# Mamba2 scan and SwiGLU feed-forward on one core: scan outputs of every second 64 tokens written with swapped feature halves, and a new order of steps

## The chip, the cores and the metric

One core of one Trainium2 chip runs the whole program. The metric is device time in microseconds (us). Engines are named as in the profile: PE is TensorE (matrix products, with PEld its weight loads), DVE is VectorE, ACT is ScalarE, POOL is GpSimd, SP is SyncE, which issues the DMAs here. Each engine executes its own instructions in the order in which the program emits them, and semaphores order the engines among each other.

## The reference, cut to what matters

```python
# x: 4 batches, 8 heads, 768 tokens, 32 features; a: decays; B, C: 16 states; chunks of 32
log_a = np.log(np.clip(a, 1e-06, 1.0))
...
    cum = np.cumsum(la, axis=-1)
    L = np.exp(cum[:, :, :, None] - cum[:, :, None, :]) * causal
    M = np.einsum('bhin,bhjn->bhij', Cc, Bc) * L
    y_intra = np.einsum('bhij,bhjd->bhid', M, xc)
    y_inter = np.einsum('bhin,bhnd->bhid', Cc, state) * np.exp(cum)[:, :, :, None]
    y[:, :, sl] = y_intra + y_inter
    state = decay_full * state + np.sum(Bx, axis=2)
...
# y as 3072 tokens x 256 features, then
rms = np.sqrt(np.mean(x * x, axis=-1, keepdims=True) + 1e-06)
xn = x / rms * rms_g
g = xn @ w_gate              # 256 x 1536
silu = g * (1.0 / (1.0 + np.exp(-g)))
return silu * (xn @ w_val) @ w_out
```

## The kernel before

**Scan.** The 768 tokens of a sequence are worked on in chunks of 64; two chunks (u = 0 and 1, 64 tokens each) make 128 tokens, and a *pair* p is two such groups (i = 0, 1), 256 tokens. There are 12 pairs and 6 *blocks* of 512 tokens (TB), so a block is two pairs. For a pair, `turn`/`turned` (L498, L514) transpose B and C, `product` (L549) multiplies C with B into g, a masked decay L is built from row and token sums (`spread` L457 by DMA, `subtract` L464, `exponential` L471, `decayed` L597), `additions` (L619) computes what the tokens add to the state (A) and `states` (L634) carries the state S on. The outputs of pairs 0 and 1 come from `first_outputs` (L658), those of all later pairs from `outputs` (L689), whose matmuls are recorded at L699. `outputs` has two stages: first C times the state ("T,S" in the profile: tiles of 32 rows by 64 columns, one for each q, that is two heads' 32 state rows, at row group 32q), then L times x ("L,xr": 64 rows by 32 columns, one for each head, row half by u). Before the change the result stands in four PSUM banks: y[2k+u] holds feature half k (128 of 256 features, one on each partition) of chunk u; the banks of k = 0 form one tile (the "y pair"), those of k = 1 are two single banks y2 and y3. The matmuls of the next pair's `additions` (`after`, "xr,Bd", L627) follow into the same banks.

**Norm.** `squares` (L733) squares y on ACT and adds the halves on POOL; `taken_out` (L751) copies y to SBUF on ACT (the copies are recorded at L763); `norm_sums` (L769), `norm_roots` (L781: Ln, then Exp, then a DMA), `spread_roots` (L792: four DMAs) and `norm_apply` (L799) make the normed tokens xn; in blocks after the first, `combine_x` (L883) makes sums of its quarters, tx.

**Feed-forward.** The weights come as float64 words (`fetch` L149, 20 pieces), and are decoded by ACT (`power` L175), DVE (`mantissa` L189) and DVE again (`weight` L198). In block 0 the first tiles of gate and value are plain products (`products_early` L831, `products_gv` L822). The rest goes by seven products in the place of eight, a tile j of 256 hidden features at a time: `product_gv` (L893) does product P.k of tile j, two matmuls of 128x256; products 1, 6, 7 and 4 accumulate in one PSUM buffer of the gate (two such buffers), 2, 5 and 3 in one of the value. After each of P.1, P.6, P.7, ACT copies the gate buffer (`taken_gv` L915, recorded at L917) before the next of them may write there; `total_gv` (L920, recorded at L923) adds copy and value buffer on DVE, `silu_gv` (L925) and `hide_gv` (L934) make the hidden features, and `product_o` (L982, recorded at L1001), `taken_o` (L1012) and `total_o` (L1019) project them with w_out, again by seven products.

**Order.** The loop over blocks is not in the code: the string `order` (L1193 to L1349) lists every step of the program, "block:kind.arguments/slot", some 1,500 of them, and the loop at L1350 executes it. Kinds are bound to functions in `first_kinds` (block 0) and `kinds` (later blocks, where the scan steps such as `y`, `sq`, `yt`, `ms`, `rs`, `xn` act on the block after). In the prediction's text `P`, `take`, `C`, `silu`, `hid` are the steps of the seven products, `o` and `O` of the projection, `pow`, `man`, `wt` of decoding the piece of that number, `row` the sums of four chunks' decays (`row_sums` L1072), `rowe` their exponent (e_sb, L1089), `turn`, `T`, `Tt` the transposition of a pair, and `table` and `exps` preloads of ACT's function table (Silu, or Ln with Exp). ACT also loads a table by itself where the next function needs another set; the profile shows that as ACT_TABLE_LOAD.

## Time and profile before

| what | value |
| --- | --- |
| three runs | 403.33, 405.25, 405.29 us (median 405.25) |
| span of the profiled execution (its own time is not listed apart from it) | 402.1 us |
| busy: PE, DVE, ACT, POOL | 394.8, 297.9, 224.5, 37.6 us |
| one pass of a 128x128 by 128x256 matmul (L911), mean of a record | 0.38 us |
| copy of a gate buffer (L917), 99 of them | 0.581 us mean |
| sum on DVE (L923), 99 of them | 0.688 us mean |
| table loads on ACT | 21 of 1.283 us |
| DMA moved | 26.99 MB |

The span is the profiled execution from its first to its last instruction. An fp32 matmul leaves two records, one for each pass. The record of a matmul is longer than the time by which the next may follow it, since they are pipelined: passes of 256 columns follow each other every 0.216 us, those of 128 every 0.11 us. "Idle before" in a group of instructions is what the engine stood still ahead of them, with the engine and line that released it.

### The profile page before, as it was taken

The page shows a single profiled execution, that of the slowest core. Times are in us where ns is not written, and L with a number is a line of the kernel's source. Part 1 is how long each engine was busy: PE and PEld are TensorE (multiplying, and loading weights), DVE is VectorE, ACT ScalarE, POOL GpSimd, SP SyncE. Part 2 cuts the span into 40 slices and gives each one's busy share as a digit, 9 for nine tenths or more (in the row PEclk, how much of TensorE's full clock was granted, in tenths as well). Part 3 has the DMA queues.
Part 4 walks back from the last instruction along what each step waited for, and adds up shares of the span by engine and source line. Part 5 has one row for each costly group of instructions (what it writes and reads, how often), then busy time and mean ns, then how long its engine had stood idle before and what let it go on. Part 6 is the DMA issues. An engine that isn't in the chain of part 4 may idle for free.

```text
span 402.1 us, 9591 instructions
## 1 busy us (share of the span) xinstructions
PE 394.8 (98%) x3881; PEld 338.9 (84%) x3881; DVE 297.9 (74%) x686; ACT 224.5 (56%) x456; POOL 37.6 (9%) x57
## 2 busy tenths in 40 slices
PE   8989999999999999999999999999999999999997
PEld 5656477888888899888899988899988899988996
DVE  6999999999477997567689467887555767366871
ACT  3989887894684362753572653482645551445410
POOL 2210010001300021200102300021200010000000
PEclk9999999999999999999999999999999999999999
DMA  9989997129012306301223700202000001100001
GB/s 110 189 248 277 178 183 236 38 42 96 2 39 67 68 22 118 79 0 17 68 74 80 104 2 0 44 30 71 27 2 2 2 9 54 52 0 2 0 2 52
DMA packets 92595, 26.99 MB, mean 67 GB/s; under 512 B 77288, under 2 KB 86376, under 8 KB 92552
## 3 DMA queue, kind: packets, MB, share of 16 engines
q1 hardware_dynamic: 88392, 26.13, 30.1%
q10 hardware_dynamic: 4160, 0.26, 0.8%
q8 instruction: 30, 0.49, 0.5%
q14 instruction: 13, 0.11, 0.1%
HBM read 22.64 MB, written 3.74 MB: 66 GB/s over the span
## 4 chain that ended last, share of the span: by engine, by line
PE 91%; SPq 3%; DMA 2%; DVE 1%; ACT 1%; issue 0%
PE gate L911 28%; PE o L1001 24%; PE val L911 21%; PE o L943 5%; PE gate L827 4%; PE y L699 3%; PE gate L837 2%; PE g L562 2%; SPq L121 1%; DMA wr<-in_moe_w_val_dram 1%; PE tp L505 1%; SPq L128 1%; DMA br<-in_B_dram 1%; PE y L627 1%; SPq L160 1%; PE ms L777 0%
## 5 line engine op out<-in xcount | busy, mean ns | idle before, releaser
L923 DVE TENSOR_TENSOR c<-val,p 128x512 f32<-128x512 f32 x99 | 67.5, 688 | 33.8 <-PE val L911 29.6
L917 ACT COPY p<-gate 128x512 f32<-128x512 f32 x99 | 57.4, 581 | 53.2 <-PE gate L911 50.4
L911 PE MATMUL gate<-tx,sw 128*128 128x256 f32 x264 | 65.8, 381 | 0.0
L932 ACT ACTIVATE c<-c 128x256 f32<-128x256 f32 x99 | 39.5, 416 | 44.5 <-DVE c L923 44.5
L911 PEld LDWEIGHTS gate<-tx,sw 128*128 128x128 f32 x264 | 49.5, 190 | 7.1 <-issue 0.3
L936 DVE TENSOR_TENSOR h<-c 128x256 f32<-128x256 f32 x99 | 41.1, 426 | 18.2 <-ACT c L932 18.2
L911 PE MATMUL val<-xn,sw 128*128 128x256 f32 x132 | 33.6, 382 | 0.5 <-DVE c L923 0.5
L911 PE MATMUL val<-tx,sw 128*128 128x256 f32 x132 | 33.6, 383 | 0.1
L911 PE MATMUL val<-xn,wgv 128*128 128x256 f32 x132 | 33.7, 382 | 0.0
L911 PE MATMUL gate<-xn,wgv 128*128 128x256 f32 x132 | 33.4, 380 | 0.0
L911 PE MATMUL gate<-tx,wgv 128*128 128x256 f32 x132 | 33.0, 381 | 0.0
L475 POOL TENSOR_SCALAR_AFFINE_SELECT L<-L 64x512 f32<-64x512 f32 x32 | 23.7, 740 | 87.0 <-ACT L L473 85.8
L1001 PE MATMUL o<-wo,h 128*128 128x128 f32 x240 | 29.9, 276 | 0.0
L1001 PEld LDWEIGHTS o<-wo,h 128*128 128x128 f32 x240 | 28.5, 192 | 0.5 <-issue 0.2
L1001 PE MATMUL o<-two,h 128*128 128x128 f32 x240 | 28.9, 276 | 0.0
L1001 PE MATMUL o<-two,s 128*128 128x128 f32 x240 | 28.9, 276 | 0.0
L911 PEld LDWEIGHTS val<-xn,sw 128*128 128x128 f32 x132 | 24.8, 190 | 4.2 <-DVE c L923 0.9
L1001 PEld LDWEIGHTS o<-two,s 128*128 128x128 f32 x240 | 28.0, 192 | 0.4 <-issue 0.2
L911 PEld LDWEIGHTS val<-tx,sw 128*128 128x128 f32 x132 | 24.7, 190 | 3.9 <-DVE c L923 0.5
L1001 PEld LDWEIGHTS o<-two,h 128*128 128x128 f32 x240 | 27.8, 192 | 0.2 <-DVE s L967 0.2
L911 PEld LDWEIGHTS gate<-tx,wgv 128*128 128x128 f32 x132 | 24.8, 190 | 3.5 <-ACT c L932 0.2
L911 PEld LDWEIGHTS val<-xn,wgv 128*128 128x128 f32 x132 | 24.8, 190 | 3.5 <-issue 0.2
(188 smaller groups left out, 614.1 us busy)
## 6 DMA issues: line engine op xcount, KB each, us to landing
L<-rowd SPq DMA_DIRECT2D x32, 128.0 KB, 3.0
xr<-in_x_dram SPq DMA_DIRECT2D x24, 128.0 KB, 4.7
wr<-in_moe_w_out_dram SPq DMA_DIRECT2D x6, 512.0 KB, 7.0
wr<-in_moe_w_val_dram SPq DMA_DIRECT2D x5, 512.0 KB, 6.4
wr<-in_moe_w_gate_dram SPq DMA_DIRECT2D x5, 512.0 KB
out_dram<-ob SPq DMA_DIRECT2D x9, 256.0 KB, 2.2
br<-in_B_dram SPq DMA_DIRECT2D x22, 64.0 KB
cr<-in_C_dram SPq DMA_DIRECT2D x22, 64.0 KB, 2.4
```

Of the source, the lines that this page charges most:

```text
L475: nc.gpsimd.affine_select(out=L[r], in_=L[r], pattern=[[0, NH], [1, HC]], compare_op=ALU.is_ge, fill=0.0, base=0, channel_multiplier=-1)
L562: nc.tensor.matmul(out=g[u, P * i:P * i + P].rearrange("p (t m) -> p t m", t=2), lhsT=T[r, i, 0, u], rhs=T[r, i, 1:3, u], start=(first and ...
L699: nc.tensor.matmul(out=y[2 * k + u][rows, (2 * n + i) * HC:(2 * n + i + 1) * HC], start=(k, u, rows.start) not in opened, stop=True, skip_ ...
L827: nc.tensor.matmul(out=gv[:, k], lhsT=w[:, t, fs], rhs=xns[0][:, t], start=(t == 0), stop=(t == 1))
L837: nc.tensor.matmul(out=gv[:, k, tk], lhsT=w[:, t, fs], rhs=yts[0][:, t, tk], start=(s == 0 and t == 0), stop=(t == 1), skip_group_check=True)
L911: nc.tensor.matmul(out=dst[:, half[w]], lhsT=lhsT, rhs=rhs, start=(k in (1, 2, 5) and w == 0), stop=True, skip_group_check=True)
L917: nc.scalar.copy(out=t, in_=Xs[j])
L923: nc.vector.tensor_tensor(out=t, in0=Zs[j], in1=a, op=ALU.add)
L932: nc.scalar.activation(out=u, in_=src[:, half[0]], func=AF.Silu)
L936: nc.vector.tensor_tensor(out=hidden_tile(blk, j)[:, c // 10 - 1, c % 10 - 1], in0=u, in1=src[:, half[1]], op=ALU.mult)
L943: nc.tensor.matmul(out=o, lhsT=hs_[blk, f // 2][:, f % 2, k // 2, (k % 2) * P:(k % 2 + 1) * P], rhs=wo[:, f], start=opens, stop=(f == NF - ...
L1001: nc.tensor.matmul(out=o[t] if apart else o[:, t * P:(t + 1) * P], lhsT=lhsT[:, t], rhs=rhs, start=(k in (1, 2, 4, 5) and j == 0 and (apar ...
```

## The change

In `outputs` the four banks change places: now the two banks of u = 1 form the y pair, and those of u = 0 are y2 and y3. For u = 1 the column strip of the PE array, and with it the PSUM partitions, are swapped by halves of 64 in both stages, and in the first stage the loop over u goes inside the loop over q. `squares` and `taken_out` follow: three squares as before, the two single banks apart and the pair at once, into a tile sq with two planes (the square roots r now use its second plane, where they had a tile of their own); four copies in the place of three, since the pair is copied in two steps of 64 partitions each, from the other half. The sums of squares need no swap, since they run over all partitions and both banks. The rest of the diff is the order string: it holds the same 1,548 steps, but from the one behind `0:man.5` on (the 91st) they stand in a new order; only the last 238 steps, from the end of block 4 on, are as before. Of the string the lines up to the first products after 60 us are kept below, and two more that the prediction speaks of.

```diff
--- before.py
+++ after.py
@@ -691,7 +691,7 @@
         first = p - n
         if n == 0:
             ps["y pair", p] = pair
-            ps["y", p] = [pair[:, 0], pair[:, 1], bank("y2", (P, 512)), bank("y3", (P, 512))]
+            ps["y", p] = [bank("y2", (P, 512)), pair[:, 0], bank("y3", (P, 512)), pair[:, 1]]
         y, s, opened = ps["y", first], st[p], set()
         width = 1 if p < 4 else 2
 
@@ -702,11 +702,11 @@
             opened.add((k, u, rows.start))
 
         for i in range(2):
-            for u in range(2):
-                for q in range(NQ):
+            for q in range(NQ):
+                for u in range(2):
                     if (2 * p) % NC == 0 and i == 0 and u == 0:
                         continue
-                    r, o = slice(32 * q, 32 * q + 32), 64 * (q % 2)
+                    r, o = slice(32 * q, 32 * q + 32), 64 * ((q + u) % 2)
                     S = state[2 * (2 * p + i) + u - 1]
                     product_y(q // 2, u, i, slice(o, o + 64),
                               lhsT=S[r].rearrange("p t d -> p (t d)"),
@@ -715,7 +715,7 @@
         for i in range(2):
             for h in range(NH):
                 for u in range(2):
-                    o = 32 * (h % 4)
+                    o = 32 * ((h + 2 * u) % 4)
                     product_y(h // 4, u, i, slice(o, o + 32), lhsT=s["x"][halves[u], i, h],
                               rhs=Ls[p][halves[u], i, h], tile_position=(HC * u, o))
         for k, p2 in enumerate(after):
@@ -724,44 +724,50 @@
                            for u in range(2)])
         del st[p], Ls[p]
 
-    def parts_of_y(p):
-        y, n = ps["y", p], 2 if p < 4 else 4
-        cols = slice(0, n * HC)
-        return n, [(0, slice(0, 2), ps["y pair", p][:, :, cols])] + [
-            (1, slice(u, u + 1), y[2 + u][:, cols].unsqueeze(1)) for u in range(2)]
+    def columns_of_y(p):
+        n = 2 if p < 4 else 4
+        half = p % 2
+        return n, slice(half * 256, half * 256 + 256) if p < 4 else slice(0, TB), slice(0, n * HC)
 
     def squares(p):
         blk, half = divmod(p, 2)
         if half == 0:
-            sqs[blk] = nrm.tile([P, TB], FP32, tag="sq", name="sq", bufs=1)
-        tk = slice(half * 256, half * 256 + 256) if p < 4 else slice(0, TB)
+            sqs[blk] = nrm.tile([P, 2, TB], FP32, tag="sq", name="sq", bufs=1)
+        n, tk, cols = columns_of_y(p)
         if p < 2:
-            sq2 = nrm.tile([P, 2, 256], FP32, tag="sq2", name="sq2", bufs=1)
+            sq2 = sqs[blk][:, 1].rearrange("p (k m) -> p k m", k=2)
             nc.scalar.activation(out=sq2, in_=ps["y", p][:, :, 0:256], func=AF.Square)
-            nc.gpsimd.tensor_tensor(out=sqs[blk][:, tk], in0=sq2[:, 0], in1=sq2[:, 1], op=ALU.add)
+            nc.gpsimd.tensor_tensor(out=sqs[blk][:, 0, tk], in0=sq2[:, 0], in1=sq2[:, 1],
+                                    op=ALU.add)
             return
-        n, parts = parts_of_y(p)
-        sq2 = nrm.tile([P, 2 * n * HC], FP32, tag="sq2", name="sq2", bufs=1)
-        for k, us, y in parts:
-            dst = (sqs[blk][:, tk], sq2)[k].rearrange("p (j u m) -> p u j m", j=n, u=2)
-            nc.scalar.activation(out=dst[:, us],
-                                 in_=y.rearrange("p u (j m) -> p u j m", j=n), func=AF.Square)
-        nc.gpsimd.tensor_tensor(out=sqs[blk][:, tk], in0=sqs[blk][:, tk], in1=sq2, op=ALU.add)
+        dst = sqs[blk][:, :, tk].rearrange("p k (j u m) -> p k u j m", j=n, u=2)
+        y = ps["y", p]
+        for k in range(2):
+            nc.scalar.activation(out=dst[:, k, 0], func=AF.Square,
+                                 in_=y[2 * k][:, cols].rearrange("p (j m) -> p j m", j=n))
+        nc.scalar.activation(
+            out=dst[:, :, 1], func=AF.Square,
+            in_=ps["y pair", p][:, :, cols].rearrange("p k (j m) -> p k j m", j=n))
+        nc.gpsimd.tensor_tensor(out=sqs[blk][:, 0, tk], in0=sqs[blk][:, 0, tk],
+                                in1=sqs[blk][:, 1, tk], op=ALU.add)
 
     def taken_out(p, copy):
         blk, half = divmod(p, 2)
         if half == 0:
             yts[blk] = nrm.tile([P, 2, TB], FP32, tag="yt", name="yt", bufs=1)
-        tk = slice(half * 256, half * 256 + 256) if p < 4 else slice(0, TB)
+        n, tk, cols = columns_of_y(p)
         if p < 2:
             for t in range(2):
                 nc.vector.tensor_scalar(out=yts[0][:, t, tk], in0=ps["y", p][:, t, 0:256],
                                         scalar1=gcol[:, t:t + 1], scalar2=None, op0=ALU.mult)
             return
-        n, parts = parts_of_y(p)
-        for k, us, y in parts:
-            copy(out=yts[blk][:, k, tk].rearrange("p (j u m) -> p u j m", j=n, u=2)[:, us],
-                 in_=y.rearrange("p u (j m) -> p u j m", j=n))
+        dst = yts[blk][:, :, tk].rearrange("p k (j u m) -> p k u j m", j=n, u=2)
+        y = ps["y", p]
+        for k in range(2):
+            copy(out=dst[:, k, 0], in_=y[2 * k][:, cols].rearrange("p (j m) -> p j m", j=n))
+        pair = ps["y pair", p][:, :, cols].rearrange("p k (j m) -> p k j m", j=n)
+        for r, there in zip(halves, halves[::-1]):
+            copy(out=dst[r, :, 1], in_=pair[there])
 
 
     xns, roots = {}, {}
...
@@ -1199,153 +1205,152 @@
         0:Tt.0.1.1 0:exp.0.1 0:turn.0.0 0:Tt.0.1.0 0:T.0.0 0:sums.0.0 0:Tt.0.0.0 0:exp.0.0
         0:turn.1.1 0:T.1.1 0:scale.1 0:Tt.1.0.1 0:fetch.2 0:Tt.1.1.1 0:cc 0:g.0.1/1 0:L.0.1
         0:turn.1.0 0:Tt.1.1.0 0:Tt.1.0.0 0:sums.1.1 0:T.1.0 0:exp.1.1 0:A.0 0:S.0 0:A.1 0:S.1
-        0:g.0.0/0 0:man.0 0:pow.0 0:L.0.0 0:pow.1 0:wt.0 0:last.1 0:man.5 0:mask.1.0/1 0:middles
-        0:Tl.1 0:sums.1.0 0:never16 0:fetch.4 0:exp.1.0 0:g.1.0/2 0:fetch.3 0:x.4 0:L.1.0 0:last.0
-        0:Tl.0 0:scale.2 0:fetch.6 0:g.1.1/0 0:fetch.7 0:man.1 0:pow.5 0:L.1.1 0:y.0/1 0:wt.5 0:sq.0
-        0:fetch.12 0:row.1 0:pow.3 0:rowout.1 0:yt.0 0:ydone.0 0:rowe.1 0:y.1/2 0:r.1 0:fetch.13
-        0:row.0 0:man.2 0:fetch.9 0:wt.1 0:early.0.0/0 0:parts.1 0:man.6 0:mask.3/1 0:sums.3 0:pow.2
-        0:wt.2 0:rowe.0 0:dT.2 0:sq.1 0:ms.0 0:yt.1 0:ydone.1 0:early.0.1 0:man.3 0:wt.3 0:mask.2/2
-        0:sums.2 0:pow.6 0:fetch.8 0:wt.6 0:man.4 0:x.2 0:exp.3 0:early.1.0/1 0:rs.0 0:norm.0 0:xn.0
-        0:pow.4 0:wt.4 0:fetch.10 0:man.7 0:dT.3 0:turn.2 0:early.1.1 0:norm.1 0:rowout.0 0:exp.2
-        1:table 0:man.9 0:silu.0 0:hid.0 0:gate.2/0 0:T.2 0:Tt.2.0 0:Tt.2.1 0:Td.2 0:pow.7
-        0:fetch.14 0:wt.7 0:tx.0 0:gg.2/1 0:L1.2.2 0:L1.2.3 0:L.2.0 0:man.8 0:gate.3/2 0:pow.9
-        0:fetch.11 0:silu.2 0:hid.2 0:pow.8 0:wt.9 0:wt.8 0:man.11 0:silu.3 0:hid.3 0:A.2 0:S.2
-        0:x.3 0:pow.11 0:gate.4/1 0:silu.4 0:hid.4 0:cw.3 0:bc.3 0:scale.3 0:man.10 0:pow.12
-        0:gate.5/0 0:silu.5 0:hid.5 0:pow.10 0:y.2/2 0:S.3 0:yt.2 0:sq.2 0:ydone.2 0:switch.1
-        0:P.2.3 0:switch.0 0:P.1.3 0:take.1.3 0:turn.3 0:T.3 0:Tt.3.0 0:Tt.3.1 0:wt.10 0:wt.11
-        0:P.1.4 0:P.6.3 0:take.6.3 0:man.12 0:Td.3 0:man.13 0:pow.14 0:gg.3/2 0:L1.3.3 0:L.3.0
-        0:L1.3.2 0:bc.4 0:scale.4 0:P.2.4 0:P.7.3 0:bc.5 0:scale.5 0:x.5 0:y.3/2 0:wt.12 0:take.7.3
-        0:C.11.3 0:P.5.3 0:silug.11.3 0:pow.13 1:S.0 0:fetch.18 0:P.4.3 1:dT.0 0:C.22.3 0:P.3.3
-        0:take.1.4 0:silug.22.3 0:cw.4 0:P.6.4 0:silu.1 0:silug.21.3 0:C.11.4 0:silug.11.4
-        0:take.6.4 0:P.5.4 0:P.7.4 1:S.1 0:sq.3 0:yt.3 0:ydone.3 1:turn.1 0:tok 0:tokout 0:wt.13
...
+        0:g.0.0/0 0:man.0 0:pow.0 0:L.0.0 0:pow.1 0:wt.0 0:last.1 0:man.5 0:fetch.7 0:fetch.9
+        0:fetch.4 0:x.5 0:mask.1.0/1 0:sums.1.0 0:last.0 0:middles 0:g.1.0/2 0:exp.1.0 0:Tl.1
+        0:g.1.1/0 0:Tl.0 0:fetch.3 0:L.1.0 0:pow.5 0:y.0/1 0:sq.0 0:L.1.1 0:fetch.6 0:row.1
+        0:rowout.1 0:rowe.1 0:man.1 0:yt.0 0:fetch.11 0:r.1 0:pow.2 0:wt.1 0:y.1/2 0:wt.5 0:sq.1
+        0:pow.4 0:early.0.0/0 0:turn.2 0:T.2 0:parts.1 0:ms.0 0:rs.0 0:never16 0:mask.3/1 0:Tt.2.0
+        0:fetch.8 0:sums.3 0:man.2 0:exp.3 0:yt.1 0:row.0 0:x.2 0:man.3 0:xn.0 0:wt.2 0:early.0.1
+        0:man.4 0:pow.3 0:dT.2 0:scale.2 0:wt.3 0:mask.2/2 0:sums.2 0:exp.2 0:rowe.0 0:wt.4 0:bc.3
+        0:man.9 0:norm.0 0:pow.9 0:man.7 0:wt.9 0:pow.7 0:Tt.2.1 0:early.1.0/1 0:early.1.1 0:norm.1
+        0:fetch.10 0:ydone.1 0:gate.3/2 0:silu.0 0:man.6 1:dT.1 0:rowout.0 0:pow.6 0:Td.2 0:bc.5
+        0:gg.2/1 0:wt.7 0:silu.1 0:L.2.0 0:hid.0 0:L1.2.3 0:L1.2.2 0:ydone.0 0:gate.2/0 0:scale.3
+        0:A.2 0:pow.8 0:wt.6 0:gate.4/1 0:man.8 0:tx.0 0:wt.8 0:silu.2 0:hid.2 0:S.2 0:gate.5/0
+        0:pow.11 0:cw.3 0:silu.3 0:hid.3 0:x.3 0:y.2/2 0:silu.4 0:pow.10 0:fetch.14 0:man.10 0:hid.4
+        0:bc.4 0:man.11 0:S.3 0:silu.5 0:hid.5 0:switch.1 0:P.2.3 0:switch.0 0:scale.4 0:sq.2 0:dT.3
+        0:wt.11 0:fetch.12 0:yt.2 0:turn.3 0:scale.5 0:T.3 0:Tt.3.0 0:P.1.3 0:Tt.3.1 0:Td.3 0:gg.3/2
+        0:wt.10 0:L.3.0 0:L1.3.2 1:table 0:L1.3.3 0:take.1.3 0:P.6.3 0:fetch.13 0:pow.12 0:x.4
+        0:y.3/2 0:take.6.3 0:P.7.3 0:pow.14 0:P.1.4 0:man.12 0:C.11.3 0:cw.4 0:wt.12 1:S.0
+        0:take.7.3 0:silug.11.3 0:pow.13 0:P.5.3 0:C.22.3 0:P.4.3 0:silug.21.3 0:fetch.16 1:S.1
+        0:hidg.21.3 0:take.1.4 0:P.2.4 0:C.11.4 0:sq.3 0:P.3.3 1:dT.0 0:C.12.3 0:P.6.4 0:hidg.11.3
+        0:man.13 0:wt.13 0:man.14 0:yt.3 0:take.6.4 0:P.5.4 0:tok 0:pow.16 0:ydone.3 0:tokout
+        0:P.7.4 1:turn.1 0:fetch.18 0:take.7.4 0:C.22.4 0:silug.22.3 0:P.1.5 0:take.1.5 0:ms.1
+        0:spread.10 0:fetch.15 0:hidg.22.3 0:P.4.4 0:P.2.5 0:wt.14 0:silug.11.4 0:silug.21.4 0:P.3.4
+        0:hid.1 0:silug.12.3 0:silug.22.4 0:pow.15 0:ydone.2 0:o.0/2 0:cw.5 0:P.6.5 0:hidg.11.4
+        0:C.11.5 0:silug.11.5 0:spread.8 0:hidg.21.4 0:P.5.5 0:spread.11 0:hidg.12.3 1:T.1 1:Tt.1.0
+        0:o.1 0:fetch.17 0:hidg.22.4 0:table.1 0:hidg.11.5 0:take.6.5 0:man.15 0:wt.15 0:exps 1:cw.2
+        0:P.7.5 0:cw.1 0:rs.1 0:rb.1 0:o.2 0:o.3 0:take.7.5 0:C.22.5 0:P.3.5 0:man.16 0:silug.22.5
+        0:C.12.4 0:wt.16 0:P.4.5 0:spread.9 0:C.12.5 0:hidg.22.5 0:o.4 0:o.5 0:xn.1 1:P.1.0 0:cw.0
+        0:pow.17 0:silug.21.5 1:P.2.0 0:tx.1 1:turn.0 0:silug.12.4 0:pow.18 0:hidg.12.4 0:silug.12.5
...
+        4:P.1.0 3:Oadd.11 3:ex.2 4:P.2.0 3:Oadd.21 4:P.1.1 3:tx 4:take.1.0 4:P.6.0 4:C.11.0 3:exps
+        4:take.1.1 4:P.6.1 4:take.6.0 4:P.7.0 4:P.5.0 4:take.7.0 4:P.4.0 4:silu.21.0 3:O.3.0 3:s4.4
...
```

More of the change, by code (lines that the diff above doesn't have):

```diff
@@ L772, in norm_sums @@
             ps["m", blk] = ms = bank("ms", (P, TB))
-            nc.tensor.matmul(out=ms, lhsT=mean, rhs=sqs[blk], start=True, stop=True)
+            nc.tensor.matmul(out=ms, lhsT=mean, rhs=sqs[blk][:, 0], start=True, stop=True)
             return
@@ L1219 @@
-        0:take.1.4 0:silug.22.3 0:cw.4 0:P.6.4 0:silu.1 0:silug.21.3 0:C.11.4 0:silug.11.4
-        0:take.6.4 0:P.5.4 0:P.7.4 1:S.1 0:sq.3 0:yt.3 0:ydone.3 1:turn.1 0:tok 0:tokout 0:wt.13
-        0:take.7.4 0:fetch.15 0:fetch.16 0:C.12.3 0:silug.12.3 0:P.2.5 0:pow.15 0:ms.1 1:dT.1
-        0:P.4.4 0:man.14 0:hidg.22.3 0:hidg.11.3 0:hidg.21.3 0:P.1.5 0:silug.21.4 0:C.22.4
-        0:take.1.5 0:silug.22.4 0:P.3.4 0:wt.14 0:pow.16 0:o.0/2 0:hid.1 0:cw.5 0:P.6.5 0:o.1
-        0:fetch.17 0:man.15 0:C.11.5 0:take.6.5 0:P.5.5 0:table.0 0:fetch.19 0:hidg.11.4 0:hidg.22.4
@@ L1225 @@
-        0:hidg.12.3 0:P.7.5 0:C.12.4 0:silug.12.4 0:take.7.5 0:wt.15 0:pow.17 0:o.2 0:o.3 0:man.16
-        0:wt.16 0:o.4 0:o.5 0:cw.1 0:P.4.5 0:man.17 0:hidg.21.4 0:hidg.12.4 0:wt.17 0:o.6 0:o.7
-        0:man.18 0:C.22.5 0:P.3.5 0:exps 0:spread.10 0:spread.8 0:sub.8 0:spread.9 0:spread.11
-        0:sub.10 0:man.19 0:rs.1 0:rb.1 1:turn.0 0:silug.11.5 0:hidg.11.5 0:pow.18 0:wt.18 0:o.8
-        0:o.9 1:two.0 1:T.1 0:pow.19 0:wt.19 1:T.0 0:C.12.5 0:silug.12.5 0:sub.11 0:hidg.12.5 0:o.10
-        0:silug.21.5 0:hidg.21.5 0:silug.22.5 0:ex.11 0:xn.1 1:P.1.1 1:take.1.1 1:P.2.1 1:P.1.0
```

241 lines of the change are left out of this document (120 added, 121 removed).

## Prediction

> **What bounds the kernel now.** I read the page's first part, its slices and its chain first, to see which engine carries the end.
>
> ```profile
> span 402.1 us, 9591 instructions
> ## 1 busy us (share of the span) xinstructions
> PE 394.8 (98%) x3881; PEld 338.9 (84%) x3881; DVE 297.9 (74%) x686; ACT 224.5 (56%) x456; POOL 37.6 (9%) x57
> ...
> DMA  9989997129012306301223700202000001100001
> ...
> PE 91%; SPq 3%; DMA 2%; DVE 1%; ACT 1%; issue 0%
> ```
>
> TensorE (PE) is busy for 98% of the span and makes 91% of the chain. The DMA row is full only in the first six slices of 10 us. Then the table of stages, whose columns after the length are busy time and count of PE, weight loads, VectorE (DVE), ScalarE (ACT) and GpSimd, clock, DMA share and GB/s:
>
> ```profile
> 0.00:25.00 25.00, 21.46 (x250) 13.14 (x250) 20.92 (x68) 16.15 (x34) 5.73 (x18) 1.00 1.03 168
> 25.00:52.00 27.00, 27.00 (x234) 15.43 (x238) 26.10 (x57) 24.69 (x39) 1.02 (x1) 1.00 0.91 221
> 52.00:68.00 16.00, 15.24 (x340) 11.72 (x330) 14.83 (x39) 13.60 (x30) 1.03 (x1) 1.00 0.90 230
> 68.00:100.00 32.00, 32.00 (x159) 27.67 (x159) 30.67 (x65) 24.43 (x44) 2.47 (x3) 1.00 0.44 68
> 100.00:145.00 45.00, 45.00 (x524) 39.64 (x523) 34.06 (x82) 26.71 (x61) 5.01 (x7) 1.00 0.19 43
> 145.00:380.00 235.00, 235.00 (x2230) 212.45 (x2229) 159.85 (x350) 116.35 (x246) 22.30 (x28) 1.00 0.16 36
> ```
>
> From 68 to 380 us PE never idles; up to 68 us DVE and ACT are within a few tenths to 2 us of full too, so there a late step on any of three engines delays PE. PE's waits say how much is left to win by order alone:
>
> ```profile
> PE r_ps L1076 <- ACT e_sb L1089: 0.9, 1, 0.9
> PE y L677 <- DVE L L601: 0.8, 1, 0.8
> PE val L911 <- DVE c L923: 0.5, 1, 0.5
> ```
>
> With the small rows below these and the restart behind each (weights are not yet in the array), PE's stops after 18 us come to 3.6 us: 0.4, 0.95 and 1.05 before 26 us, 0.4 at 55.5, 0.6 and 0.2 at 65.0 and 67.0. So the change can gain by shorter work on PE and at most about 3.6 us by order, and loses wherever the new order makes PE wait.
>
> **Part 1, the matmuls of y (L699).** One pair of the second to sixth block, in the timeline (start, length, engine, line):
>
> ```profile
> 51.56 0.69 PE L699 MATMUL y<-T,S 32*64 32x64 f32 x32
> ...
> 52.19 0.69 PEld L699 LDWEIGHTS y<-L,xr 64*32 64x32 f32 x64
> 52.19 0.86 PE L699 MATMUL y<-L,xr 64*32 64x64 f32 x64
> ```
>
> The matmuls of state and C (T,S) hold PE from 51.56 to 52.19. Their 32 records (two for a matmul) start four at once, one in each row group of 32, at 0, 107, 165, 223, 282, 340, 398 and 457 ns. Each uses 64 of 128 columns, so half the array stands idle. The new order issues both 64-token halves of one row group behind each other, and the swap puts them on different column halves. The kernel has that form already, in the product of C and B for the later pairs (L562: row groups outside, two column halves inside, 32*64 tiles): there eight records start within 46 ns, the next eight at 160, then every 109 ns, for 128 columns streamed. So T,S should go eight at a time, at 0, 107, 165 and 223 ns by its own steps, the last at 223+46=269 instead of 477 ns: 0.21 us less. Three of the ten pairs begin a sequence and have 24 records (last start at 360 ns); they should end near 245 ns, 0.115 us less. Sum 7x0.21+3x0.115 = **-1.8 us**. What follows (L,xr, 0.64 us a pair) keeps its tiles except for their column strip; its first 32 records start in groups of eight, its second 32 one per 16.6 ns, and I can't tell from the trace whether a changed column order helps those. Bounds: 0 if nothing packs, -4 if the second half of L,xr also runs at the pace of its first (0.2 us a pair).
>
> [...]
>
> **Part 2, ScalarE.** The squares stay three a pair group. The copies out of PSUM (L763) go from three to four: where before one copy took the two banks of the pair over all partitions, two copies of 64 partitions now swap the halves. ACT's time goes by elements per partition in its rows (128x128 0.296, 128x256 0.408, 128x512 0.600 us), so one more 0.408 twice and 0.600 four times, +3.2 us on ACT, all beside PE except in the 50s. The new order also changes table switches: in the two instruction lists I count 29 table loads against 21, eight more, several of them with no use (a set loaded and replaced by the next instruction). One costs:
>
> ```profile
> 105.83 0.64 ACT L473 ACTIVATE L<-L 128x512 f32<-128x512 f32 x1
> 106.49 1.28 ACT L932 ACT_TABLE_LOAD   x1
> 107.78 0.42 ACT L932 ACTIVATE c<-c 128x256 f32<-128x256 f32 x1
> ```
>
> So +10.3 us on an engine that is 56% busy. [...] Two of the new loads stand in the chains of norms of blocks 2 to 4 (Ln, then Exp, each with its set); before, one block had that at 265 us and PE did not stop. In the new order some 22 to 30 projections of block 1 and 2 (about 0.5 us each) lie between the sums and the first product of the next block, for a chain of some 8 us (loads 2.6, Ln 0.37, Exp 0.31, two DMAs of 2 to 3 us). I take **0** for all of ACT's part after 110 us; bounds 0 and +4.5 (rival B).
>
> **Part 3, the order up to 60 us.** Every step from the 90th moves, DMA issues on SyncE too. The weights of fetch.3 (256 KB of w_val) go from 3.25 to 4.56 MB in the queue's order; the DMA engines are full then, and the transfer that stood at 4.56 MB before landed at 29.6 us, fetch.3 at 23.15. It is needed by man.3 (DVE). row.0 (PE) now waits for its bank until ACT has done the Ln of rs.0, which stands behind pow.4, whose fetch.4 should land near 25.9 instead of 22.2. I walked both orders with the durations of the rows: near 20 us the new one is 2.6 us ahead (the wait at L1076 is gone), then it loses 1.5 to 2 us on DVE behind fetch.3 and about as much at row.0; y of pair 2 comes at 51.7 (before 51.56). Then turn.3 has four yt copies, three squares and a Silu ahead of it on ACT, and the first P.6 waits for a table load (1.28) and a 0.58 copy: P.6.3 near 59.3. At the same work PE is 1.2 us later than before, with two pairs' savings in it (0.4), so 1.6 by itself. The walk adds full durations where rows overlap (three yt copies take 0.69 us in the timeline, 1.0 by their sum), so I take **+1.0**; bounds -1.5 (all stops of before between 22 and 67 us gone, half of them kept gone) and +3.
>
> **Part 4, the products after 67 us.** Products 1, 6 and 7 of a tile go into one PSUM buffer, each copied by ACT (take, L917) before the next may write. From the last pass of a product, ACT starts its copy after 0.417 us; it takes 0.585 and PE starts 0.053 later: 1.055. With one other product between, PE is free again after 0.216+4x0.216=1.079. So it fits by 0.02, but the weights are not preloaded: in before's stops PE lost another 0.104 where it started 0.053 after the release, 0.060 where the release led by 0.097, and nothing from 0.227 on. A lead of 0.077 costs 0.08. Before keeps at least 0.26 of slack in all such loops; the new order has 17 with exactly one product between and 4 tighter by a few tens of ns: 17x0.08+4x0.11 = **+1.8 us** (bounds 0 and 2.5). What waits behind is only PE itself.
>
> **Sum.** -1.8+0+1.0+1.8 = +1.0 us, a span of 403.1. The profiled execution has no separate time; its span of 402.1 lies 1.2 to 3.2 below the three runs (403.33, 405.29, 405.25), so I add the change to their median, 405.25: **406.2 us**, with 404 to 408.5 for this case alone.
>
> **Rivals.**
> A, the order packs as well as before: the 0.08 at each tight loop is hidden because the weight load needs no restart when PE never stops in full, and the startup is even. Then -1.8, and some 0.8 of the waits on c at 65 to 67 us go: 402.6. For it: no PE stop in before after 67 us; against it: the leads above.
> B, table loads become the late link: three of the new loads stand right in front of copies that a product of the same buffer waits for (take.6.5 of block 0, 1.28; take.7.5 behind a load, Ln and Exp, 1.96; take.1.1 of block 4, 1.28). It decides where PE reaches that product less than a load plus a copy, 1.87 us, after the one before. All exposed: 406.2+4.5 = 410.7, slower. For it: ACT 85 to 91% busy up to 68 us; against: it has 8 us idle of 32 in 68 to 100.
> C, T,S does not pack (the halves of one row group run in series): the change then does not do what it says, 406.2+1.8 = 408.0. Against it: L562.
>
> **Chances.** Forecast 0.42, A 0.29, B 0.21, C 0.06, 0.02 beyond. A measurement here tells about 0.5%, 2 us, from no change. Faster by more: A, 0.29. Within: most of the forecast, 0.37. Slower: B, C, the forecast's upper end and the rest, 0.34. For 8 in 10 the range runs from A's 402.6 less half a microsecond to B's 410.7: 402.1 to 410.7.
>
> **What would show it.** T,S starting eight at once and y from its first record to the next product 0.1 to 0.2 us shorter (part 1); 29 table loads and PE waits on p (L923 of the new kernel) after 67 us near 0 in the wait view but PE idle of about 0.1 at each tight loop (part 4); the first P.6 near 59.3 us (part 3). Wrong if PE's busy time up to 68 us falls by more than 2 us, or if one wait on ACT exceeds 1 us after 68.

## The result: 1.6% slower, and the profile after

The changed kernel takes 411.24 us (median of 6 runs, 409.39 to 413.11), the one before 405.27 beside it: a ratio of 1.0157, 95% interval 1.0131 to 1.0182. On another chip it was 409.12 to 403.56, 1.0121 (1.0098 to 1.0145). Forecast was 406.2, with a range up to 410.7. The profiled execution is one of 411.39 us, with a span 7.6 us over that of before. First its page, from span, engines, granted clock and chain:

```profile
span 409.7 us, 9573 instructions
## 1 busy us (share of the span) xinstructions
PE 397.3 (97%) x3881; PEld 337.0 (82%) x3881; DVE 294.7 (72%) x686; ACT 236.6 (58%) x470; POOL 35.3 (9%) x57
...
PE 74%; ACT 9%; DVE 5%; DMA 4%; SPq 4%; issue 3%; POOL 0%; DVEq 0%; ACTq 0%; POOLq 0%
```

PE's share of the chain falls from 91 to 74%: others now end the waits. ACT has 14 more records, 8 of them table loads (29 for 21). The table of stages (after the length: PE, weight loads, DVE, ACT, POOL busy, clock, DMA share, GB/s) says where:

```profile
25.00:52.00 27.00, 24.53 (x193) 13.62 (x192) 23.69 (x55) 21.82 (x34) 0.00 (x0) 0.94 0.85 176
52.00:68.00 16.00, 14.41 (x347) 10.67 (x345) 15.12 (x40) 15.62 (x31) 0.74 (x1) 1.00 0.95 244
68.00:100.00 32.00, 31.66 (x155) 26.72 (x154) 29.88 (x64) 27.15 (x53) 0.73 (x1) 1.00 0.44 90
100.00:145.00 45.00, 45.00 (x491) 38.83 (x490) 36.16 (x82) 24.24 (x53) 5.88 (x8) 1.00 0.24 49
145.00:380.00 235.00, 231.66 (x2260) 206.32 (x2244) 151.72 (x342) 125.64 (x256) 21.51 (x28) 1.00 0.15 35
```

Before, PE was full from 25 to 52 us and from 68 on. Now it stands 2.5 us in the first stretch, whose clock is 0.94, and 3.3 us between 145 and 380. PE's waits name the places:

```profile
PE r_ps L1082 <- ACT sq L792: 2.5, 1, 2.5
PE y L699 <- issue: 1.7, 1, 1.7
...
PE gate L917 <- ACT p L923: 1.1, 2, 0.8
PE o L1007 <- DVE h L977: 0.9, 1, 0.9
PE tp L505 <- ACT yt L767: 0.5, 1, 0.5
PE ms L783 <- POOL sq L751: 0.5, 1, 0.5
```

Three of these are read below: row.0, which waits for the square roots (sq at L792 is r, in the second plane of sq); a stop inside y without any releaser; and a projection that waits for DVE. And the matmuls of y, first records of a pair as shown of before:

```profile
52.94 0.49 PE L699 MATMUL y<-T,S 32*64 32x64 f32 x32
53.35 0.80 PE L699 MATMUL y<-L,xr 64*32 64x64 f32 x60
```

T,S holds PE for 0.41 us where it held it for 0.63. Its 32 starts lie in four groups of eight, the last at 0.270 us (0.477 before), in the pairs with 24 records at 0.244 (0.360). The part of the change that was its core does what was forecast, to 1 ns a pair: -1.8 us over the ten pairs. The loss comes from elsewhere.

### The profile page after: what moved, and what is told of

Same layout as the page of the kernel before. It is cut to its first block, busy times and chain, and to the rows that moved or that the text cites. A ratio compares the mean times of both kernels' runs of the same rounds, so it can differ in the third digit from the quotient of the medians.

```text
span 409.7 us, 9573 instructions
## 1 busy us (share of the span) xinstructions
PE 397.3 (97%) x3881; PEld 337.0 (82%) x3881; DVE 294.7 (72%) x686; ACT 236.6 (58%) x470; POOL 35.3 (9%) x57
## 4 chain that ended last, share of the span: by engine, by line
PE 74%; ACT 9%; DVE 5%; DMA 4%; SPq 4%; issue 3%; POOL 0%; DVEq 0%; ACTq 0%; POOLq 0%
PE gate L917 27%; PE val L917 19%; PE o L1007 17%; PE o L949 5%; DMA wr<-in_moe_w_gate_dram 2%; PE y L699 2%; SPq L121 1%; ACT e L183 1%; ACT e L182 1%; PE g L562 1%; DMA sq<-roots 1%; DMA br<-in_B_dram 1%; SPq L128 1%; SPq L160 1%; ACT e L185 1%
## 5 line engine op out<-in xcount | busy, mean ns | idle before, releaser
L917 PE MATMUL gate<-tx,sw 128*128 128x256 f32 x264 | 67.3, 385 | 1.1 <-ACT p L923 1.1
L917 PEld LDWEIGHTS gate<-tx,sw 128*128 128x128 f32 x264 | 48.1, 190 | 10.9 <-ACT p L923 4.5
L475 POOL TENSOR_SCALAR_AFFINE_SELECT L<-L 64x512 f32<-64x512 f32 x32 | 22.3, 697 | 156.3 <-ACT L L473 155.0
L917 PE MATMUL gate<-tx,wgv 128*128 128x256 f32 x132 | 33.9, 384 | 0.0
L1007 PE MATMUL o<-wo,h 128*128 128x128 f32 x240 | 31.4, 277 | 0.0
L1007 PE MATMUL o<-two,s 128*128 128x128 f32 x240 | 31.2, 277 | 0.2
L1007 PE MATMUL o<-two,h 128*128 128x128 f32 x240 | 29.8, 275 | 0.9 <-DVE h L977 0.9
L1007 PEld LDWEIGHTS o<-two,s 128*128 128x128 f32 x240 | 29.1, 192 | 1.1 <-DVE s L973 0.3
```

The source lines that it names most:

```text
L475: nc.gpsimd.affine_select(out=L[r], in_=L[r], pattern=[[0, NH], [1, HC]], compare_op=ALU.is_ge, fill=0.0, base=0, channel_multiplier=-1)
L917: nc.tensor.matmul(out=dst[:, half[w]], lhsT=lhsT, rhs=rhs, start=(k in (1, 2, 5) and w == 0), stop=True, skip_group_check=True)
L1007: nc.tensor.matmul(out=o[t] if apart else o[:, t * P:(t + 1) * P], lhsT=lhsT[:, t], rhs=rhs, start=(k in (1, 2, 4, 5) and j == 0 and (apar ...
```

## The experiments

All ratios are to the kernel before on the same chip, with 95% intervals. The experiments ran on several chips, so kernels are compared by these ratios.

**1. Layout and order apart: y_only, order_only.** y_only has the new functions and the old string:

```diff
-        0:g.0.0/0 0:man.0 0:pow.0 0:L.0.0 0:pow.1 0:wt.0 0:last.1 0:man.5 0:fetch.7 0:fetch.9
+        0:g.0.0/0 0:man.0 0:pow.0 0:L.0.0 0:pow.1 0:wt.0 0:last.1 0:man.5 0:mask.1.0/1 0:middles
...
```

> The new functions (banks, swap, loop order, squares, four copies) with the steps in the old order. Theory (the layout saves what the trace of the changed kernel shows for the matmuls of T and S, last start 0.270 for 0.477 us, 0.244 for 0.360, ten pairs, and the loss lies all in the new order): 405.3 - 1.8 = 403.5 us, PE never waiting after 70 us. Rival (the fourth copy and its half partitions on ACT push later steps back): 405 or more, with PE waits on ACT behind the copies.

Measured: 402.64 us, 0.9959 (0.9944 to 0.9975): by the ratio 1.65 us faster than before. By ratio it is the fastest kernel of this study.

order_only is the other half, the diff of the change without its part above the string:

> The old functions (old banks, three copies, loop order i, u, q) with the steps in the new order. Theory (order costs, layout gains): the changed kernel's 411.2 + 1.8 = 413 us. Rival (the new order was made for the new layout and the two belong together: the loss comes from the layout's copies in that order): 409 or less.

Measured: 408.58, 1.0098 (1.0074 to 1.0123). So the order alone costs 4.0 us (from the ratio), less than expected and within the rival's bound. The layout that saves 1.65 us in the old order saves nothing in the new one: 1.0121 and 1.0157 stand against 1.0098, 1 to 2.4 us more, and the lower of the two lies within the noise. The rival has a point: the two interact. Experiments 4 and 5 show where.

**2. Early and late apart: early_new, late_new.** New functions; the string is cut behind `0:o.0` (near 80 us), and the rest is what the other string still has to do, in its order. For late_new, against the string of before:

```diff
-        0:o.0/2 0:hid.1 0:cw.5 0:P.6.5 0:o.1 0:fetch.17 0:man.15 0:C.11.5 0:take.6.5
+        0:o.0/2 0:spread.10 0:hid.1 0:cw.5 0:P.6.5 0:hidg.11.4 0:C.11.5 0:silug.11.5 0:spread.8
...
```

> New functions; the steps in the new order up to the first projection step of block 0 (o.0, near 80 us), the rest in the old order. Theory (loss up to 74 us about 2.8 us: the 2.5 us wait of PE on the square roots at 26.9 us, a lower clock for 4 us behind it, three waits on ACT at 56 to 60 us; after that nothing but the gain of y): 405.3 - 1.8 + 2.8 = 406.3, between 405.5 and 407.5. Rival (all of the loss is made in the start, since everything later runs behind late steps): 410 or more.

> New functions; the steps in the old order up to o.0 of block 0, then what is left in the new order. Theory (stops after 74 us: 9.5 us in the trace of the changed kernel against 3.1 before, so 6.4 more): 405.3 - 1.8 + 5 to 6.4 = 408.5 to 410. Rival (they are followers of the late start): 404 or less.

Measured: early_new 404.62, 1.0012 (0.9996 to 1.0029); late_new 407.44, 1.0082 (1.0057 to 1.0108). Against y_only (402.64) the new start costs 2.0 us and the new rest 4.8. They add up: 402.64+2.0+4.8 = 409.4, which is 1.014 of before on that chip; the changed kernel has 1.0121 and 1.0157 on two others. In PE's records after 74 us, the time by which one start is later than the pace of the passes sums to 3.3 us in y_only (3.1 before) and 8.4 in late_new: the late loss is stops of PE, all of it.

**3. The start: pow4_later.** Only change to the changed kernel:

```diff
-        0:pow.4 0:early.0.0/0 0:turn.2 0:T.2 0:parts.1 0:ms.0 0:rs.0 0:never16 0:mask.3/1 0:Tt.2.0
+        0:early.0.0/0 0:turn.2 0:T.2 0:parts.1 0:ms.0 0:rs.0 0:pow.4 0:never16 0:mask.3/1 0:Tt.2.0
```

> The changed kernel with one step moved: the exponents of weight piece 4 (pow.4 on ACT) behind the square roots of block 0 (rs.0). Theory: PE's wait of 2.5 us at row.0 goes, for ACT no longer stands idle waiting for that piece's DMA while the sums of squares are ready, and with it the fall of the granted clock to 0.5 right behind the wait: -3 to -4 us, 407.5 to 408.5, if the weights of piece 4 don't come late in turn. Rival 1 (the clock falls from another cause, at a fixed time): -2.5 at most, clock still 0.5 to 0.73 between 28 and 32 us. Rival 2 (the next late link, the sums and masks of pair 2 or piece 3 on DVE, takes its place): 0 to -1.

Measured: 408.89, 1.0128 (1.0111 to 1.0145). The stretch that follows, in the changed kernel and then in pow4_later:

```profile
26.00:28.00 2.00, 0.85 (x38) 0.36 (x36) 0.98 (x3) 1.77 (x3) 0.00 (x0) 1.00 0.74 171
28.00:30.00 2.00, 0.68 (x3) 0.68 (x4) 0.76 (x3) 1.97 (x5) 0.00 (x0) 0.73 0.97 297
30.00:32.00 2.00, 2.00 (x7) 1.69 (x7) 1.95 (x3) 1.97 (x4) 0.00 (x0) 0.50 0.98 332
32.00:34.00 2.00, 2.00 (x43) 1.28 (x41) 1.98 (x5) 0.67 (x2) 0.00 (x0) 0.91 1.17 293
```

```profile
28.00:30.00 2.00, 2.00 (x44) 1.32 (x42) 1.93 (x4) 1.97 (x4) 0.00 (x0) 1.00 0.95 300
30.00:32.00 2.00, 1.41 (x17) 0.68 (x4) 0.65 (x2) 1.94 (x4) 0.00 (x0) 1.00 1.13 318
32.00:34.00 2.00, 1.29 (x6) 1.17 (x7) 1.74 (x4) 1.97 (x5) 0.00 (x0) 1.00 0.58 125
```

Above, PE is idle for 2.5 us, and then runs "busy" at half the clock: 7 records in 2 us. Below the long stop is gone, two of 0.5 us (a decay's exponents on ACT, L455) and 0.8 us (weights of the early products on DVE, L201) stand in its place, and the clock stays at 1.00. So rival 2 took about half of the wait, and the theory is right on the clock. The time can't be told from that of the changed kernel (1.0121 and 1.0157); -3 to -4 us were expected. Of ten runs of the changed kernel on two chips, the mean granted clock was 1.0 in three (407.9 to 409.4 us), 0.996 in five (410.4 to 411.4 on the first chip, 409.4 on the other) and 0.992 in two (413.1 and 411.6). In none of the four runs of pow4_later was it below 1.0. So one fall costs 1 to 2 us, by the times of these runs. Why it comes in some executions only is not shown. In the clock records of the changed kernel's two traces a fall behind a stop lasts 3.413 us. In the second trace (after_again) the falls begin at 28.45, 318.58 and, behind PE's last work, 410.74 us, 85.0 and 27.0 times that length apart; in the first at 28.93 and 411.22, 112.0 times. Whether the place of a stop against those times decides was not tested.

**4. The stop inside y: y_apart, y_together, phase, pair_fetch_before, pair_fetch_inside.** In the changed kernel the y of pairs 10 and 11 stand beside each other. The timeline:

```profile
316.75 0.49 PE L699 MATMUL y<-T,S 32*64 32x64 f32 x32
...
317.17 0.42 PE L699 MATMUL y<-L,xr 64*32 64x64 f32 x22
...
319.32 0.67 PE L699 MATMUL y<-L,xr 64*32 64x64 f32 x42 [1.73 <-issue]
```

PE stops in the middle of 64 like matmuls, and nothing releases it. The page lists a queue "q8 instruction" with 30 packets and 0.49 MB, 16 KB each; in the trace's DMA packets one of them begins at 316.69.

y_apart moves the second. y_together was meant to do the opposite to the kernel before, but its kernel has the new functions: it is y_only with `4:y.1` right behind `4:y.0`. The edit of y_apart:

```diff
-        4:silu.12.3 4:y.0 4:y.1 4:hid.21.3 4:P.1.5 4:C.12.2 4:hid.12.3 4:P.2.5 4:sq 4:hid.11.3 4:s.3
+        4:silu.12.3 4:y.0 4:hid.21.3 4:P.1.5 4:C.12.2 4:hid.12.3 4:P.2.5 4:y.1 4:sq 4:hid.11.3 4:s.3
```

> The changed kernel with one step moved: the y of the last pair, which stood right behind the y of the pair before it, goes two products (P.1.5 and P.2.5 of block 4) later. Theory (96 small matmuls in a row use up PE's instructions faster than the next 16 KB of them are fetched, and PE stands for 1.8 us near 318 us): that stop goes, -1.5 to -1.8 us. Rival (the second y waits for data that the profile doesn't name, so it waits wherever it stands): 0 to -0.5.

> The kernel before with one step moved: the y of the last pair right behind that of the pair before it in block 4. Theory of the instruction fetch: PE stops inside the second y for 1 to 2 us with no releaser in the profile. Rival: no such stop.

pair_fetch_before is the same program as y_together, run on another chip. phase (96, in the changed kernel) and pair_fetch_inside (24, in pair_fetch_before) add small matmuls to `idle`; for phase:

```diff
             nc.tensor.matmul(out=ps["idle"], lhsT=warm[:, 0:P], rhs=warm, start=True, stop=True)
+        for k in range(96):
+            nc.tensor.matmul(out=ps["idle"][:, 0:4], lhsT=warm[:, 0:P], rhs=warm[:, 0:4],
+                             start=True, stop=True)
```

> The changed kernel with 96 extra matmuls of 4 columns (results unused) in PE's idle time of the first microseconds, so that all later instructions of PE lie 192 further on in the stream, and a fetch of 16 KB of instructions falls elsewhere. Theory (the stop of 1.8 us at 318 us is PE running out of instructions, since a fetch begins inside the two y stages that stand together; instructions come to use 2.4 to 2.6 us after their fetch begins): it goes or shrinks, and the fetch nearest to it no longer begins inside the pair; -1.3 to -1.8 us, unless another fetch now falls into another y. Rival (it waits for data): the stop stays in its place.

> New functions, old order, with the y of the last pair right behind that of the pair before it. In the old order the fetch of instructions falls 0.5 us ahead of the first of these two (309.5 for 309.95 us). Theory (PE stops only where a fetch begins inside the pair, since the instructions come to use 2.4 to 2.6 us later): no stop inside the pair. Rival (two y stages in a row always stop, or the second waits for data): a stop over 0.5 us inside the second.

> The same, with 24 extra matmuls of 4 columns (results unused) in PE's idle time of the first microseconds, two instructions each, so that all later fetches of 256 instructions fall 48 instructions earlier in the stream, which is 208 later counted from the one before: about 1.1 us behind the start of the pair. Theory: a stop of 1.2 to 1.9 us inside the second y, ending 2.4 to 2.6 us after the fetch begins, with the same steps in the same order. Rival (data): no stop, as without the extra matmuls.

Measured: y_apart 409.43, 1.0144 (1.0126 to 1.0163). The stop is gone from the y stage, but a product behind it now waits 0.8 us for the hidden features of its buffer: no clear gain. y_together took 404.87 us and pair_fetch_before 403.56, one run each; the first has no stop, the second one of 0.42 us, and neither is what was expected. phase took 411.33, 1.0205 (1.0167 to 1.0243), and is slower than the changed kernel. Its trace is of its longest run (415.95 us): the stop stays (1.46 us), and a new one of 3.6 us that ends at 67.9 appears in the y stage of pair 3, with half the clock behind it; in its other five runs the mean clock was 1.0. The extra matmuls moved the fetches, but not to where the expectations had them: in phase the fetch near the pair begins 1.4 us behind its start, and in pair_fetch_inside (405.48 us, one run) 2.1 us behind it, at the pair's end. But phase moved the place of the stop: PE stops behind the 182nd of the pair's 192 records, and behind the 150th in the five other traces of the changed kernel and of kernels made from it that stop there (the changed kernel twice, exps_once, pow4_later, loops_apart). Those 32 records are 64 instructions (a weight load and a matmul each), and 192 were added: by this shift I put the fetches 256 instructions apart, an estimate. In the changed kernel 253 of PE's records lie between two fetches on average (7,335 in 29 stretches; register and branch instructions are not among them). What settles it is all kernels together, with the time of the nearest fetch from the packets. The stop is counted from when the next matmul was due; the idle time in the timeline is 0.1 us less.

| kernel (two y stages together) | fetch begins, from the pair's start | stop inside | goes on, after the fetch began |
| --- | --- | --- | --- |
| pair_fetch_inside | +2.14 us (the pair's end) | none | - |
| y_together | -0.60 | none | - |
| order_only (old layout) | -0.13 | none | - |
| late_new | -0.09 | 0.63 us | 2.65 us |
| pair_fetch_before (the program of y_together) | -0.04 | 0.42 | 2.30 |
| exps_once (below) | +0.96 | 1.37 | 2.36 |
| loops_apart (below) | +1.04 | 1.54 | 2.45 |
| changed kernel, two traces | +1.10, +1.14 | 1.54, 1.83 | 2.38, 2.63 |
| pow4_later | +1.33 | 1.82 | 2.43 |
| phase | +1.41 | 1.46 | 2.35 |

The same steps wait or don't by where the fetch falls (y_together and pair_fetch_before are even one program), and PE goes on 2.3 to 2.7 us after it began. By these eleven traces it is a shortage of instructions and not of data. It is also one part of the interaction: order_only has the same pair, with T,S 0.42 us longer in all and the fetch just ahead of it, and no stop.

**5. The norm chain: exps_once.** In the changed kernel three table loads stand in a row ahead of the square roots of block 4.

```diff
-        3:s.5 3:s2.1 3:s2.2 2:table 3:spread.3 3:sub.3 3:rs 3:rb 3:s3.2 3:O.5.5 3:s3.0 3:s2.0
+        3:s.5 3:s2.1 3:s2.2 3:spread.3 3:sub.3 3:exps 3:rs 3:rb 3:s3.2 3:O.5.5 3:s3.0 3:s2.0
...
-        4:P.1.0 3:Oadd.11 3:ex.2 4:P.2.0 3:Oadd.21 4:P.1.1 3:tx 4:take.1.0 4:P.6.0 4:C.11.0 3:exps
+        4:P.1.0 3:Oadd.11 3:ex.2 4:P.2.0 3:Oadd.21 4:P.1.1 3:tx 4:take.1.0 4:P.6.0 4:C.11.0 2:table
```

> The changed kernel, with two preloads of ACT's table moved: the set with Ln and Exp is loaded right before the square roots of block 4, the preload of Silu that stood there goes behind the first products of block 4. ACT's Ln and Exp then share one load where three stood in their chain (26 loads in all for 29). Theory (the wait of 1.0 us at 285 us is the end of a chain: copies of y, squares, sums, Ln, Exp, two DMAs, xn on DVE, h on DVE, projection on PE; the loads lie in it): that wait goes, -0.8 to -1.0 us. Rival (the loads lie beside waits and cost nothing, the chain is late by the DMAs or by DVE's own work): 0.

DVE in the changed kernel, and then in exps_once:

```profile
283.05 1.42 DVE L810 SCALAR_TENSOR_TENSOR xn<-yt,gcol,sq 128x512 f32<-128x512 f32 x2 [2.94 <-DMA sq<-roots]
284.38 0.42 DVE L977 TENSOR_TENSOR h<-h 128x256 f32<-128x256 f32 x1
```

```profile
279.98 1.40 DVE L810 SCALAR_TENSOR_TENSOR xn<-yt,gcol,sq 128x512 f32<-128x512 f32 x2
281.30 0.41 DVE L977 TENSOR_TENSOR h<-h 128x256 f32<-128x256 f32 x1
```

The normed tokens come without a wait, and so does h behind them; PE's wait "o <- DVE h" of 0.9 us is no longer among its waits. In time it can't be seen: 409.64, 1.0139 (1.0120 to 1.0159), beside 1.0121 of the changed kernel on the same chip (after_again); in three of its four runs the clock was 0.996.

The run does not show that the loads are the cause, for order_only has the same three loads and no wait of PE for h. Its copies are shorter (three take 0.99 us, in the changed kernel four take 1.83), and its roots come out of ACT 0.74 us earlier; but xn comes 2.57 us earlier. The rest is in the packets of the four DMAs that spread the roots (sq<-roots). In the changed kernel all but the last eight packets of 512 bytes are through at 280.82; a fetch of PE's instructions begins at 280.84 and takes 0.88 us, and the eight end from 281.77 on, the last at 282.17. It is so in all six traces in which a fetch falls into this spread (the changed kernel twice, late_new, pow4_later, y_apart, loops_apart): the first of the eight ends 0.06 us behind the fetch, and xn waits 2.3 to 2.9 us. In order_only and in phase (in this order below) no fetch falls there, no packets stay behind, xn waits 0.8 and 1.0 us, and PE does not wait for h.

```profile
280.48 1.42 DVE L804 SCALAR_TENSOR_TENSOR xn<-yt,gcol,r 128x512 f32<-128x512 f32 x2 [0.82 <-DMA r<-roots]
```

```profile
287.14 1.41 DVE L813 SCALAR_TENSOR_TENSOR xn<-yt,gcol,sq 128x512 f32<-128x512 f32 x2 [1.01 <-DMA sq<-roots]
```

phase has all steps of the changed kernel, three loads and four copies included. So loads and copies alone make xn 1.0 us late without cost to PE, and PE's wait comes with the fetch. exps_once took loads away and with them brought the spread 2 us forward, clear of the fetch, so it can't tell the two apart. The fetch is the other part of the interaction too.

> The changed kernel once more, as the one that the next three are compared with on the same chip. Both theories: 1.3 to 1.6% above the kernel before; where the granted clock falls in the wait of PE near 28 us, by 1.5 to 2 us more.

**6. The tight loops: loops_apart.** 13 loops with only one product between copy and next use were opened by putting a product one PE step later, one of them:

```diff
-        4:take.1.1 4:P.6.1 4:take.6.0 4:P.7.0 4:P.5.0 4:take.7.0 4:P.4.0 4:silu.21.0 3:O.3.0 3:s4.4
+        4:take.1.1 4:take.6.0 4:P.7.0 4:P.6.1 4:P.5.0 4:take.7.0 4:P.4.0 4:silu.21.0 3:O.3.0 3:s4.4
...
```

> The changed kernel, with 13 of the 18 products that follow the copy of their own buffer by one product only put one step of PE later. Theory (each such loop costs 0.08 to 0.10 us since the weights can't be loaded ahead of the release): 13 of the stops of 0.079 or 0.104 us go, -1.0 to -1.3 us. Rival (the later product delays the sums behind it, and new waits take the gain): 0 or slower.

Measured: 413.26, 1.0249 (1.0222 to 1.0276): much slower. A product put off puts off its own copy, and the next product on that buffer then waits (at four places of the new string no product is left between): PE's waits on p go from 1.1 us (2) to 4.0 (7). The experiment doesn't price the loops. The records of the changed kernel do, without an experiment behind them: at 18 such loops PE loses 0.079 or 0.104 us each time, as worked out from before.

**7. Repairs together, and the better version: three_fixes, swap_only, best.** three_fixes is the changed kernel with the edits of pow4_later and exps_once, and with the first y of the pair two products ahead of the second:

```diff
-        4:P.6.2 4:P.3.3 4:C.11.2 4:take.6.2 4:L 4:P.5.2 4:P.7.2 4:take.7.2 4:P.4.3 4:silu.21.3
+        4:P.6.2 4:P.3.3 4:C.11.2 4:take.6.2 4:L 4:P.5.2 4:P.7.2 4:take.7.2 4:P.4.3 4:silu.21.3 4:y.0
...
-        4:silu.12.3 4:y.0 4:y.1 4:hid.21.3 4:P.1.5 4:C.12.2 4:hid.12.3 4:P.2.5 4:sq 4:hid.11.3 4:s.3
+        4:silu.12.3 4:y.1 4:hid.21.3 4:P.1.5 4:C.12.2 4:hid.12.3 4:P.2.5 4:sq 4:hid.11.3 4:s.3
```

> The changed kernel with three repairs: pow.4 behind the square roots of block 0; the table with Ln and Exp loaded once ahead of the square roots of block 4; the y of pair 10 two products earlier, so that two products stand between it and that of pair 11. Theory (the losses add up and each has its own cause): the stop of 2.5 us at 28 us (in part replaced by 1.3 us of others), the wait at 285 us (0.4 to 1.0) and the stop at 318 us (1.5 to 1.8) go, and no clock falls remain: 1.2 to 1.5% above the kernel before becomes 0.5 to 0.9%; the tight loops (2.3 us) and the start's other waits stay. Rival (late steps follow one another, so that a repaired wait comes back at the next): over 1.0%.

Measured: 406.54, 1.0066 (1.0046 to 1.0086). Its PE waits:

```profile
PE gate L843 <- DVE wgv L201: 0.8, 1, 0.8
PE gate L917 <- DVE h L866: 0.7, 1, 0.7
PE gate L917 <- ACT p L923: 0.6, 2, 0.4
PE ms L783 <- POOL sq L751: 0.5, 1, 0.5
PE gate L843 <- ACT L L455: 0.5, 1, 0.5
```

The three stops are gone, the mean clock was 0.999 or 1.0 in all six runs, and about half of the loss with them, as expected. That the three causes add up is not shown: alone, none of the repairs could be told from the changed kernel (1.0128, 1.0139, and 1.0144 for y_apart). The other half stays: the tight loops and the smaller waits of the table.

swap_only takes the loop over u out of that over q again:

```diff
-            for q in range(NQ):
-                for u in range(2):
+            for u in range(2):
+                for q in range(NQ):
```

> Old order of steps, new functions, but u outside q again in the loop of T and S: the swap without the new loop order. If the loop order is what packs the halves: starts by fours, last start at 0.477 us. If the swap alone is enough, since the queue looks far enough ahead: eights, 0.27 us.

Measured: one run, 403.50 us (before: 403.69 on that chip); the last T,S start is at 0.270 us, as with the new loop order. The swap does it alone; how far the queue looks ahead, no run shows.

best is y_only with one ACT step of the start moved:

```diff
-        0:fetch.12 0:row.1 0:pow.3 0:rowout.1 0:yt.0 0:ydone.0 0:rowe.1 0:y.1/2 0:r.1 0:fetch.13
+        0:fetch.12 0:row.1 0:rowout.1 0:yt.0 0:ydone.0 0:rowe.1 0:pow.3 0:y.1/2 0:r.1 0:fetch.13
```

> New functions, old order, and one step moved in the start: the exponents of weight piece 3 (pow.3 on ACT, which waits 1.7 us for its DMA) behind the exponents of the row sums (rowe.1), for which PE waits near 25 us. Theory: PE's wait of 0.3 to 0.9 us there goes, 0.3 to 0.9 us less than the new functions in the old order (0.9959 of before), so 0.993 to 0.995. Rival (weights of piece 3 come late on DVE in turn): 0.996 or more.

Measured: 402.75, 0.9982 (0.9966 to 0.9997): the wait on e_sb goes, and PE waits 0.9 us for the sum of squares next (ms <- POOL sq). No gain over y_only, and less than expected.

## Why the prediction was wrong, point by point

- **Part 1, T,S, -1.8 us: right.** 0.269 and 0.245 us were forecast for the last starts, 0.270 and 0.244 measured; y_only gains 1.65 us (1.0 to 2.3 by its interval). The second half of L,xr didn't change (0.642 us in all). In the changed kernel's pair at 52.94 us eight records of T,S start within 46 ns and the next eight from 0.106 us on; before, four started within 20 ns and the next four from 0.107 us on.
- **Part 2, "I take 0 for all of ACT's part after 110 us": too low, but not for the loads alone.** The rows were right (29 loads of 1.283 us; four copies), but the work was set against ACT's idle share and not against the one chain in which it stands. In the norm of block 4, three loads and four copies make xn 1.0 us late in phase, and PE feels nothing of it; with a fetch of instructions in the spread of the roots xn is 2.3 to 2.9 us late, and PE waits 0.3 to 0.9 us in the two traces of the changed kernel. The wait for block 2's sums of squares at 150 us (0.5 us) stands behind the copies too, but order_only has 0.3 of it with three; no run took it away. Rival B named three loads in front of copies, and none of these was the place.
- **Part 3, +1.0 us up to 60 us: mis-sized.** early_new says +2.0. The walk found the wait at row.0 "about as much" as 1.5 to 2 us and then took off part of it for overlapping rows; it is 1.9 and 2.5 in the two traces of the changed kernel. A fall of the granted clock to 0.5 behind such a stop (1 to 2 us more in most runs) wasn't weighed at all. Stops of 1.9 to 2.6 us came with it in four traces (the changed kernel twice, order_only, exps_once), and one of 2.3 us (y_apart) did not.
- **Part 4, the tight loops, +1.8 us: right in size, as far as records go.** 0.079 and 0.104 us a loop at 18 loops; no run took the loops away without adding other waits.
- **"What waits behind is only PE itself": this step failed.** It put all of the new order after 67 us but the loops at nothing. Between the products stand projections and y. late_new loses 4.8 us where 1.8 was forecast; beside the loops there are PE waits on h (0.7), the sums (0.5), a gate copy at 79 us (0.4), and the stop inside y (0.6 here, 1.5 to 1.8 in the changed kernel). With the start, -1.65+2.0+4.8 = +5.2 us stands in the place of +1.0; measured were 4.9 and 6.4 by the two ratios, the larger where the clock fell in five of six runs.
- **The instruction fetch was in no rival.** In the changed kernel's two traces the two y stages that stand together stop for 1.83 and 1.54 us, with a fetch begun 1.14 and 1.10 us behind their start. And with a fetch in the spread of the roots xn waits 2.9 and 2.3 us there, and PE for h behind it 0.9 and 0.3 us. order_only has neither; this is where the layout, a gain in the old order, loses its gain in the new one. How much of the 1 to 2.4 us it explains was not measured.

## What to carry to other kernels

Price an added instruction by the chain in which it stands, not by its engine's idle share: ACT is idle for 42% of the span, and three loads and a copy more still made the norm 1.0 us late. Before calling that the cause of a wait, look at what else moved: here it was a fetch of instructions. A new order that looks as full as the old one can still lose its time in many small stops; list for each buffer what stands between the release and the next use, and when a long stop or a burst of small matmuls is added, count a slower clock (here 0.5 for 3.41 us) and the instruction fetch (here stops of 0.42 to 1.83 us in two y stages together) as possible followers. Measure a change of layout in the old order first: alone it was the better kernel.
